# Another start address for the split left operands of a matmul chain

## The chip, the cores and the metric

The kernel runs on one core of one Trainium2 chip. The metric is the device time of one execution in microseconds. Every operand named here lies in the on-chip memory SBUF, 128 partitions wide; an address below is the byte within a partition.

## The reference

Attention between a long sequence and a short state, in both directions, followed by a two-layer network with a Mish activation. All is in float32.

```python
# x: (8, 8, 512, 64), state: (8, 8, 32, 64), w_in: (512, 2048), w_out: (2048, 512)
scores  = scale * x @ state^T;   xread = softmax(scores) @ state
scores2 = scale * state @ x^T;   sread = softmax(scores2) @ x
t   = concat([xread, sread], axis=2) -> (8 * 544, 512)
h   = t @ w_in
g   = h * tanh(log1p(exp(h)))
out = g @ w_out
```

## The kernel before, in words

A float32 product is made of three faster ones: each operand is split into a high part (a copy rounded to the type float32r) and a low part (the rest, a subtraction), and high x high, high x low and low x high are added in PSUM. The left operand is the one that is loaded into TensorE as weights (128 columns), the right one streams past it. In the trace a load is an LDWEIGHTS on the row PEld, and the streaming a MATMUL on PE.

Batch 0 is computed while the weights arrive, in an order written out as a table; batch 1 follows in a loop over eight slots of d_ff. In both, the second product (h's activation times w_out) takes 1024 columns of left operands a slot, in the tiles `gh` and `gl` of `high_g` (line 547), and streams 512 columns of w_out a matmul.

From batch 2 on the second product is done with seven products instead of eight (Winograd's form of Strassen's method). The 512 tokens of a batch are two halves p, the state rows of all batches (key "s") are one. A step is one slot j of one half: six batches of 16 steps and 8 steps of state rows, 104 in all. `combine_g` (line 662) makes the seven left operands of a step: four sums on VectorE into the tile `s`, two rounding copies on ScalarE (three blocks out of the activation tile `gu`, four out of `s`) into `gh`, and two subtractions on VectorE into `gl`. It runs one step ahead of `products` (line 684), which issues 7 x 3 matmuls of 128 x 128 weights and 256 columns, for each product on `gh`, `gh`, `gl`. The right operands are the combined parts of w_out, in the tiles `wo`, `wt23` and `wt4`. Between the steps the first product of the next batch is issued (`gemm1`: left `swh`, `swl`, right `ah`, `al`, 512 columns), and parts of the attention. The order of the steps and of what comes between them is set by lists that the program builds before it begins; on TensorE, VectorE and ScalarE instructions are issued as written.

Where the tiles lie: `gh` and `gl` have two buffers each. Since the tiles of batches 0 and 1 under the same tags are 1024 columns wide (`W`), each buffer has 4096 bytes. The two of `gh` begin at bytes 183,552 and 187,648, the two of `gl` at 191,744 and 195,840: byte 256 after a multiple of 512. So does every block of 128 columns in them. The tiles `swh` and `swl` also lie at byte 256 of 512, the right operands `wo`, `wt23`, `wt4`, `ah`, `al` and `srT` at byte 0. Batch 1 is different in one thing: its `ah` and `al` are in buffers of the tag `gu`, at byte 256.

Of the kernel before, what the change touches and what calls it, by code (L numbers as in the profile page):

```python
# [10 lines left out]
F32R = mybir.dt.float32r  # L11
# [6 lines left out]
P = 128  # L18
# [23 lines left out]
W = 1024  # L42
# [4 lines left out]
def as_f32(ap):  # L47
    return ap.bitcast(F32)
# [41 lines left out]
def state_attention_mish_kernel(ctx, tc, x_turned, x, state_wide, state, w_in, w_out, out):  # L90
# [6 lines left out]
    pool = ctx.enter_context(tc.tile_pool(name="pool", bufs=2))  # L97
# [564 lines left out]
    def combine_g(step, between=lambda: None):  # L662

        u = units.pop(step)
        key = "_".join(str(i) for i in step)
        s = pool.tile([P, 4, P], F32, tag="h", name=f"s_{key}", bufs=1)
        a21, a11, a22, a12 = (u[:, i] for i in range(4))
        dve.tensor_add(s[:, 0], a21, a22)
        dve.tensor_sub(s[:, 2], a11, a21)
        dve.tensor_sub(s[:, 1], s[:, 0], a11)  # L670
        dve.tensor_sub(s[:, 3], a12, s[:, 1])
        gh = pool.tile([P, 7, P], F32R, tag="gh", name=f"gh_{key}")
        gl = pool.tile([P, 7, P], F32R, tag="gl", name=f"gl_{key}")
        for to, of in ((slice(0, 3), u[:, 1:4]), (slice(3, 7), s)):
            act.copy(gh[:, to], of)
        between()
        for to, of in ((slice(0, 3), u[:, 1:4]), (slice(3, 7), s)):
            dve.tensor_sub(gl[:, to], of, as_f32(gh[:, to]))
        parts[step] = gh, gl
# [149 lines left out]
    for step in STEPS.split():  # L829
        what, i = re.fullmatch(r"([a-zA-Z]+)(\d*)", step).groups()  # L830
# [14 lines left out]
    key = 1  # L845
# [47 lines left out]
    for b in base:  # L893
        for j in range(4 if b == "s" else SLOTS):
            at = {2: j - LAG, "s": (-8, -5, -3, 0)[j % 4]}.get(b, min(2 * j - 8, 5))
# [25 lines left out]
    for k in range(-LAG, len(steps)):  # L921
        if k == INORDER:
            dve.on = act.on = True
        if 0 <= k < len(steps) - 1:
            combine_g(steps[k + 1], lambda: advance(k, 0))
# [3 lines left out]
        if k < 0:  # L929
            j = pending[0][1][0] // 2  # L930
            second()
            if k == -LAG:
                whole(sw_slice(2, 2, kept=kept.pop(0)))
                load_kept()
            if k == -1:
                atts[3] = attention(3)
                aTs[3] = atts[3]["aT"]
                whole(atts[3]["sc"](0))
                running.append((3, atts[3]["pieces"]()))
                xss[3] = load_x(3)  # L940
            combine_w_out(j)
            if k == -1:
                combine_g(steps[0])
            continue
        beside, loads, begun = [], [], []
        for what, b in visits.get(k, ()):
            if what[:2] == "sw":
                i = int(what[2])
# [25 lines left out]
        key, j, p = steps[k]  # L974
# [41 lines left out]
```

## Time and profile before

| what | us |
|---|---|
| median of 3 runs | 643.89 (641.83 to 643.98) |
| the profiled execution, device time | 642.11 |
| its span, first to last instruction | 640.3 |
| PE busy (matmul) | 625.7 |
| PEld busy (weight load, runs beside PE) | 539.2 |
| DVE busy (VectorE) | 492.6 |
| ACT busy (ScalarE) | 355.9 |

The durations of single matmuls in the profile overlap: a matmul's shown time includes its way through the array, and the next one starts before it has ended. The pace of a stream of matmuls is therefore read from their starts or from the length of a piece divided by its count, not from the mean time of one. All operations have line 82, that of a helper which records them; groups are told apart by their tiles. Buffer numbers are left out of the names.

### The profile page before, as it was taken

How to read it: one execution, taken by the hardware profiler on the slowest of the kernel's cores; microseconds unless marked ns; L12 is line 12 of the kernel's file. 1: busy time of each engine (PE TensorE's matmuls, PEld its weight loads, DVE VectorE, ACT ScalarE, POOL GpSimd, SP SyncE). 2: the span in 40 equal slices, each digit the busy share in tenths (PEclk: the TensorE clock that was granted, in tenths of full speed). 3: DMA queues.
4: the chain of work that ended last, by engine and by line, in shares of the span. 5: the costliest groups of instructions: out<-in, count | busy, mean ns of one | idle time of the engine just before them, and what ended most of it. 6: DMA issues, size and time to landing. Idle time of an engine off the chain costs nothing.

```text
span 640.3 us, 13377 instructions
## 1 busy us (share of the span) xinstructions
PE 625.7 (98%) x5308; PEld 539.2 (84%) x5308; DVE 492.6 (77%) x1077; ACT 355.9 (56%) x703; POOL 0.7 (0%) x6
## 2 busy tenths in 40 slices
PE   7999998999999999999999999999999999999996
PEld 5776776777778888888898888888899898899996
DVE  5989999875767676878688776878588867666685
ACT  4999773452457544654456455754465444545442
POOL 0000000000000000000000000000000000000000
PEclk9999999999999999999999999999999999999999
DMA  8977715212352243213332243224322212103100
GB/s 322 418 268 277 263 71 168 93 69 97 132 198 79 87 165 133 99 39 126 149 118 93 82 157 132 105 94 157 118 79 77 100 67 100 67 29 137 68 34 34
DMA packets 23774, 81.67 MB, mean 128 GB/s; under 512 B 4000, under 2 KB 8480, under 8 KB 18208
## 3 DMA queue, kind: packets, MB, share of 16 engines
q1 hardware_dynamic: 23424, 80.56, 34.6%
q8 instruction: 42, 0.69, 0.5%
q10 hardware_dynamic: 288, 0.26, 0.1%
q14 instruction: 20, 0.16, 0.1%
HBM read 63.50 MB, written 13.11 MB: 120 GB/s over the span
## 4 chain that ended last, share of the span: by engine, by line
PE 68%; DVE 11%; ACT 3%; issue 2%; DMA 2%; SPq 1%; DVEq 0%; ACTq 0%
PE acc L82 36%; PE ph L82 19%; PE swp L82 4%; PE ph_s L82 4%; PE acc_s L82 3%; DVE gl L82 2%; DVE s L82 2%; DVE o L82 1%; PE srp L82 1%; DVE swl L82 1%; DVE al L82 1%; ACT gh L82 1%; SPq L376 1%; PE sc L82 1%; DMA w_in<-w_in_kept 1%
## 5 line engine op out<-in xcount | busy, mean ns | idle before, releaser
L82 PE MATMUL acc<-wo,gh 128*128 128x256 f32 (+1 forms) x1024 | 230.4, 314 | 0.0
L82 PEld LDWEIGHTS acc<-wo,gh 128*128 128x128 f32 x1024 | 169.3, 190 | 28.5 <-issue 14.9
L82 PE MATMUL acc<-wo,gl 128*128 128x256 f32 (+1 forms) x512 | 158.5, 310 | 0.7 <-DVE gl L82 0.7
L82 PE MATMUL acc<-wt,gh 128*128 128x256 f32 x576 | 112.5, 283 | 0.1
L82 ACT CAST gh<-s 128x512 fp32r<-128x512 f32 x96 | 59.4, 619 | 85.3 <-DVE s L82 85.2
L82 PEld LDWEIGHTS acc<-wo,gl 128*128 128x128 f32 x512 | 97.4, 190 | 6.1 <-DVE gl L82 0.9
L82 PEld LDWEIGHTS acc<-wt,gh 128*128 128x128 f32 x576 | 89.7, 192 | 0.2 <-issue 0.2
L82 PE MATMUL acc<-wt,gl 128*128 128x256 f32 x288 | 82.9, 288 | 0.6 <-DVE gl L82 0.2
L82 PE MATMUL ph<-ah,swh 128*128 128x512 f32 (+1 forms) x260 | 80.7, 393 | 2.5 <-ACT swh L82 1.4
L82 PE MATMUL ph<-al,swh 128*128 128x512 f32 (+1 forms) x260 | 79.1, 387 | 0.0
L82 PE MATMUL ph<-ah,swl 128*128 128x512 f32 (+1 forms) x260 | 78.9, 387 | 0.0
L82 DVE TENSOR_TENSOR gl<-gu,gh 128x384 fp32r<-128x384 f32 x96 | 52.2, 544 | 34.2 <-ACT gh L82 34.2
L82 ACT CAST gh<-gu 128x384 fp32r<-128x384 f32 x96 | 49.4, 515 | 49.6 <-PE acc L82 48.0
L82 ACT ACTIVATE gu<-ph 128x256 f32<-128x256 f32 x192 | 61.0, 385 | 23.6 <-PE ph L82 23.2
L82 DVE TENSOR_TENSOR gl<-s,gh 128x512 fp32r<-128x512 f32 x96 | 66.0, 688 | 6.6 <-ACT gh L82 6.6
L82 DVE TENSOR_TENSOR swl<-swp,swh 128x512 fp32r<-128x512 f32 (+1 forms) x72 | 41.9, 623 | 22.3 <-ACT swh L82 22.2
L82 PEld LDWEIGHTS acc<-wt,gl 128*128 128x128 f32 x288 | 55.2, 192 | 3.1 <-DVE gl L82 2.5
L82 PEld LDWEIGHTS ph<-al,swh 128*128 128x128 f32 x260 | 48.4, 188 | 10.4
L82 PEld LDWEIGHTS ph<-ah,swl 128*128 128x128 f32 x260 | 48.4, 188 | 10.3
L82 PEld LDWEIGHTS ph<-ah,swh 128*128 128x128 f32 x260 | 45.1, 189 | 12.5 <-ACT swh L82 2.6
L82 ACT CAST swh<-swp 128x512 fp32r<-128x512 f32 (+1 forms) x72 | 35.3, 544 | 31.7 <-PE swp L82 31.7
L82 DVE TENSOR_TENSOR s<-gu 128x128 f32<-128x128 f32 x192 | 47.0, 286 | 5.5 <-ACT gu L82 3.3
(95 smaller groups left out, 714.3 us busy)
## 6 DMA issues: line engine op xcount, KB each, us to landing
w_in<-w_in_kept SPq DMA_DIRECT2D x24, 1024.0 KB, 5.0
wir<-in_w_in_dram SPq DMA_DIRECT2D x16, 512.0 KB, 10.3
wor<-in_w_out_dram SPq DMA_DIRECT2D x16, 512.0 KB, 9.4
x<-in_x_dram SPq DMA_DIRECT2D x8, 1024.0 KB, 4.8
out_dram<-o SPq DMA_DIRECT2D x32, 256.0 KB, 2.2
xT<-in_x_turned_dram SPq DMA_DIRECT2D x7, 1024.0 KB, 6.3
w_in_kept<-w_in SPq DMA_DIRECT2D x8, 512.0 KB, 9.8
e2T<-e2b SPq DMA_DIRECT2D x128, 32.0 KB, 1.9
```

Of the source, the lines that this page charges most:

```text
L82: made = method(*args, **kwargs)
L376: nc.sync.dma_start(e2T[s * NS:(s + 1) * NS, c].rearrange("t u g n -> t (u g n)"), turned[c * NS:(c + 1) * NS, s * 2 * P:(s + 1) * 2 * P])
```

## The change

The two tiles of `combine_g` are made 1024 columns wide, as the tiles of batches 0 and 1 are, and the 7 x 128 columns that are used begin at column 80 in `gh` and at column 48 in `gl`. With four bytes a column and buffers at byte 256 of 512, the seven blocks of `gh` then begin at byte 64 of 512 (256 + 320 = 512 + 64) and those of `gl` at byte 448 (256 + 192). No instruction is added, removed or moved on any engine or queue, and no other tile has another address.

```diff
@@ def combine_g(step, between=lambda: None):
-        gh = pool.tile([P, 7, P], F32R, tag="gh", name=f"gh_{key}")
-        gl = pool.tile([P, 7, P], F32R, tag="gl", name=f"gl_{key}")
+        gh, gl = (
+            pool.tile([P, W], F32R, tag=t, name=f"{t}_{key}")[:, at:at + 7 * P].rearrange("p (i n) -> p i n", n=P)
+            for t, at in (("gh", 80), ("gl", 48)))
```

## Rows read from the trace of the kernel before

**Rows 1.** Top of the page: span, busy us of each engine.
```profile
span 640.3 us, 13377 instructions
...
PE 625.7 (98%) x5308; PEld 539.2 (84%) x5308; DVE 492.6 (77%) x1077; ACT 355.9 (56%) x703; POOL 0.7 (0%) x6
```
**Rows 2.** Busy time by stretch: stretch, its us, engines, granted clock, DMA share, GB/s.
```profile
235.00:315.00 80.00, 79.90 (x710) 71.02 (x708) 61.00 (x149) 43.67 (x97) 0.00 (x0) 1.00 0.31 116
570.00:600.00 30.00, 30.00 (x253) 30.00 (x252) 23.52 (x61) 15.32 (x30) 0.00 (x0) 1.00 0.30 103
```
**Rows 3.** Chain that ended last, in order of time: start us, us, what.
```profile
303.56 2.75 PE ph L82 x12
306.31 5.03 PE acc L82 x42
...
602.05 7.56 PE acc L82 x63
...
615.37 18.02 PE acc_s L82 x150
```
**Rows 4.** Timeline, 226.4 to 227.4 us: start us, us, engine, line, what.
```profile
226.61 0.28 PE L82 MATMUL acc<-wt,gl 128*128 128x256 f32 x1
...
226.97 0.28 PE L82 MATMUL acc<-wo,gl 128*128 128x256 f32 x1
226.97 0.31 PEld L82 LDWEIGHTS acc<-wo,gh 128*128 128x128 f32 x2
```
**Rows 5.** Timeline of PE in batch 1, 512 columns a matmul.
```profile
104.23 0.39 PE L82 MATMUL acc<-wo,gl 128*128 128x512 f32 x1
...
104.91 0.39 PE L82 MATMUL acc<-wo,gl 128*128 128x512 f32 x1
```
**Rows 6.** Groups from 225.9 to 228 us: count, busy us, mean ns, idle before.
```profile
L82 PEld LDWEIGHTS acc<-wo,gh 128*128 128x128 f32 x6 | 0.9, 192 | 0.0
...
L82 PE MATMUL acc<-wt,gh 128*128 128x256 f32 x6 | 1.2, 283 | 0.0
```
**Rows 7.** Timeline of PE, first and ninth matmul of a stretch behind a wait.
```profile
221.12 0.40 PE L82 MATMUL acc<-wt,gh 128*128 128x256 f32 x2
...
222.07 0.28 PE L82 MATMUL acc<-wo,gl 128*128 128x256 f32 x1
```
**Rows 8.** Groups of that stretch, 221.1 to 222.1 us.
```profile
L82 PE MATMUL acc<-wo,gh 128*128 128x256 f32 x4 | 0.8, 281 | 0.0
...
L82 PEld LDWEIGHTS acc<-wo,gh 128*128 128x128 f32 x5 | 0.8, 189 | 0.0
```
**Rows 9.** Groups from 225.64 to 225.7 us, batch 3's first product and what follows.
```profile
L82 PE MATMUL ph<-ah,swl 128*128 128x512 f32 x1 | 0.4, 389 | 0.0
L82 PE MATMUL acc<-wo,gh 128*128 128x256 f32 x1 | 0.3, 277 | 0.0
```
**Rows 10.** Tiles gh and gl: ns min/median/max; below, who waited (us, times).
```profile
L82 PE MATMUL acc<-wt,gh x576: 277/283/356, 183.8 to 609.2; 128*128 128x256 f32 x192
L82 ACT CAST gh<-s x96: 613/620/625, 170.5 to 605.0; 128x512 fp32r<-128x512 f32 x96
L82 DVE TENSOR_TENSOR gl<-gu,gh x96: 495/551/559, 170.6 to 605.1; 128x384 fp32r<-128x384 f32 x96
L82 DVE TENSOR_TENSOR gl<-s,gh x96: 677/691/694, 171.2 to 605.6; 128x512 fp32r<-128x512 f32 x96
...
  PEld acc L82: 3.4, 11
```
**Rows 11.** Timeline of PE, eight transposes of 128 columns.
```profile
519.52 1.04 PE L82 MATMUL srTp<-ident,srds 128*128 128x128 f32 x8
```
**Rows 12.** Groups from 222.6 to 224.1 us, the beginning of batch 3's first product.
```profile
L82 PE MATMUL ph<-ah,swh 128*128 128x512 f32 x2 | 0.6, 396 | 0.0
```
**Rows 13.** The page's groups: VectorE's sums ahead of gh and gl.
```profile
L82 DVE TENSOR_TENSOR s<-gu 128x128 f32<-128x128 f32 x192 | 47.0, 286 | 5.5 <-ACT gu L82 3.3
```
**Rows 14.** Groups from 98 to 140 us, batch 1's first product.
```profile
L82 PE MATMUL ph<-ah,swh 128*128 128x512 f32 x16 | 4.9, 389 | 0.0
```

## The prediction, made before the changed kernel ran

> **What bounds the kernel now.** I read the page's totals first, then the busy time by stretch, the chain of waits, the timeline of TensorE, and last the view of the tiles gh and gl. The totals [rows 1] show PE busy for 98% of 640.3 us, DVE for 77%, ACT for 56%. An average says little, so the stretches [rows 2]: from 235 to 315 us PE is busy 79.90 of 80 us and DVE 61.00, and from 570 to 600 us PE all of it, with a granted clock of 1.00 in both, the upper of its two levels (2.4 GHz). In batches 2 to 7 and in the state rows, PE is the only engine without air. The chain of waits agrees [rows 3]: from 303.56 us it runs on PE alone, in pieces of the first and of the second product, and its last piece of matmuls is 150 of the second product in 18.02 us. So the time of this part is a count of matmuls times their pace.
>
> **The pace.** 150 matmuls in 18.02 us are 120.1 ns each; 42 in 5.03 us are 119.8, and 63 in 7.56 us 120.0 [rows 3]. In the timeline the first matmul on gl comes every 0.36 us, three matmuls [rows 4]. A 512-column matmul of batch 1 with the same left tiles comes every 0.68/3 = 227 ns [rows 5]. The difference, 107 ns, is what 256 columns cost; 120 - 107 = 13 ns per matmul are something else. Every one of these matmuls is paired with a weight load of 128 columns that runs under the matmul before it: in [rows 4] a load starts with the matmul ahead of it, and it shows 192 ns where the pace is 120 [rows 6].
> [...]
>
> That the 13 ns are not fixed is shown by the matmuls that are not in the steady run. From 221.12 us, just behind a wait, eight matmuls go from 221.12 to 222.07 us, 119 ns each in the view's hundredths [rows 7], and in that stretch the loads show 189 ns and the matmuls 281 [rows 8], against 192 and 283 in the steady stretch [rows 6]. The first 256-column matmul behind a 512-column one shows 277 ns [rows 9]. The shortest on these tiles is 277, the median 283 [rows 10]. Of a matmul's shown time a constant part is its way through the array: 283 goes with a pace of 120, and 389 with 227, so 163 and 162 ns. By that, 277 is a pace of 114, and 281 one of 118. Same shapes, same addresses: what differs is how the load's and the matmul's reads fall against each other. That is what makes a change of address worth a forecast at all.
>
> **The change, part by part.** It adds no instruction, removes none, and moves none: each engine's order is the same. Tiles gh and gl of batch 2 on become 1024 wide and use columns 80 to 975 and 48 to 943. Their slots were already 4096 bytes, because batches 0 and 1 put 1024 columns there, so no other tile shifts. The left operand of 104 steps x 21 = 2184 matmuls (six batches of 16 steps and 8 steps of state rows; seven products of three matmuls a step) starts at byte 64 or 448 of a 512-byte row of addresses where it started at 256. The right operands stay at 0.
> - Writes of gh by ACT and of gl by DVE: same shape, other start. The rows of gh<-s, gl<-gu and gl<-s range from 613 to 625, 495 to 559 and 677 to 694 ns [rows 10]. I take zero. Bounds: their spread, at most 64 ns on a DVE op. It is hidden by PE: DVE has 24% of air from 235 to 315 us [rows 2]; were that gone, a step's 0.06 us would be 104 x 0.06 = 6 us. I put nothing of this in the sum.
> - The weight loads and the matmuls under them: the whole effect. No row has a 128-column load of these products from byte 64 or 448, so I bound it. Best row: 277 ns, 6 ns below the median. 2184 x 6 = 13.1 us less. Lower still is the row of the eight transposes (srTp): 1.04 us less the 0.163 of the way through the array, by eight, is 110 ns each, with a load of 128 columns each [rows 11]; they are transposes of 128 columns, so this is the far end: 2184 x 10 = 21.8 us. Worst row: the first two 512-column matmuls of a first product, on ah and swh, have a mean of 396 where the settled one has 389 [rows 9, 12], 7 ns more: 2184 x 7 = 15.3 us more.
> - Value taken: 4 ns less, halfway between the drifting stretch (2 ns less) and the first matmul behind a long one (6 ns less), since both are the same instruction as the one in question, and neither is nearer. 2184 x 4 = 8.7 us. About 1 in 20 of these matmuls stands behind a wait and would not gain; that is 0.4 us, left within the range.
> - How much arrives at the end: all of it, as long as PE stays the bound. One step is 21 x 120 = 2.52 us of PE; DVE's part of it is four sums of 0.286 [rows 13] and the two subtractions of 0.551 and 0.691 [rows 10], 2.39 us. With 116 ns PE needs 2.44, still above DVE in a run of steps without a first product between. At 114 ns it is 2.39, and DVE would be late next, at the gl that opens a product; the present waits there are 3.4 us in 11 times [rows 10]. In batches 2 to 7 the first product gives DVE room between (2.75 us before two steps, [rows 3]), so I take no loss at 4 ns. What lies behind the last matmul (633.4 to 640.3 us) stays.
>
> Sum: the profiled execution took 642.11 us (span 640.3). 642.11 - 8.7 = 633.4. The median of the three runs shown, 643.89, is 1.8 above it, so 635.2: **635 us**.
>
> **The rivals.**
> *Same.* The start address does not matter, and the pace has 120 for a reason that lies elsewhere. For it: batch 1 takes its right operands (ah, al) from slots at byte 256 where the other batches take them from byte 0, with the left ones at 256 in both; the 16 matmuls of its first product in the row show 389 ns [rows 14], and the settled row of batch 3's shows 389 too [rows 9]. That is a move of 256 bytes between the two reads that did nothing. If the pattern repeats in 64 bytes, 64, 256 and 448 are one place. Against it: 277, 281 and 283 for one kind of instruction [rows 8 to 10] say the reads do get into each other's way. Result 643.9, give or take the 2 us of the runs.
> The Trainium skill (TensorE: Matmul & The Clock Gate, "Step-by-step: what each phase is for") says that PE has two independent read ports and that loading the next weights takes no read bandwidth from the running matmul. By that rule this change does nothing and this rival holds; the trace speaks against it so far as loads and matmuls lengthen together [rows 6, 8].
> *Slower.* The two reads meet more often than now. Place: the load of the next gh or gl under a running matmul. Price: the matmul takes the 7 ns more that rows of the first product show [rows 12], 2184 x 7 = 15 us, 659 us. It decides when the new start makes the moving read wait for one more of these steps per load; half of it, 3 ns, gives 650. For it: 396 occurs with the same kind of operands, and a high part and a low part now have different starts, so the run of loads has three distances and no longer one. Against it: these 396 stand only until the stream has settled, and 256-column matmuls settle below.
> *Faster, by more.* The meeting goes away wholly: 114 ns or less. 2184 x 6 gives 630.8, with the transposes' 110 it would be 622 less what DVE then holds up, some 626.
>
> **How the numbers follow.** About 0.5% (3.2 us) is what a measurement of this kernel can tell from no change. Gain of 3.2 to 11 us (2 to 5 ns): 0.36. Gain over 11 us: 0.16. Same: 0.32. Slower by over 3.2 us: 0.16. So faster 0.52, same 0.32, slower 0.16. The likeliest is faster, its own range 628 to 640. The range 628 to 646 leaves out the gains over 16 us (0.06) and the losses over 2 us above the median (0.14 at most).
>
> **What would show it.** Right: the 150 matmuls at the end in 17.4 us instead of 18.02, a median of 279 for the matmuls on gh and gl, loads of 188 instead of 192 ns, first-product rows unchanged at 389 to 396, and waits of PE for gl of no more than 5 us. Same would show 18.02 and 283 again. Slower would show 286 or more. It would be wrong in its reason, though right in its number, if the pace stayed at 120 and waits went instead, or if ACT's and DVE's rows for gh and gl changed by more than their spread.

## The result, and the profile after

| | us |
|---|---|
| the kernel before, median of 4 runs | 643.50 (641.83 to 643.98) |
| the changed kernel, median of 4 runs | 636.61 (635.38 to 637.03) |
| ratio, with its 95% interval | 0.9894 (0.9871 to 0.9918) |
| profiled execution of the changed kernel | 637.03, span 635.2 |

The change takes 6.9 us off. The top of the page, span and busy us of each engine:

```profile
span 635.2 us, 13377 instructions
...
PE 617.3 (97%) x5308; PEld 529.2 (83%) x5308; DVE 492.5 (78%) x1077; ACT 356.0 (56%) x703; POOL 0.7 (0%) x6
```

Against [rows 1], matmuls are 8.4 us less busy and weight loads 10.0 us; VectorE and ScalarE have the work they had. Then the view of the tiles gh and gl (ns min/median/max; the last two lines are who waited for them, us and times):

```profile
L82 PEld LDWEIGHTS acc<-wt,gh x576: 186/188/191, 185.2 to 604.6; 128*128 128x128 f32 x192
L82 PE MATMUL acc<-wt,gh x576: 276/276/358, 185.3 to 604.7; 128*128 128x256 f32 x192
L82 ACT CAST gh<-s x96: 612/620/624, 172.0 to 600.8; 128x512 fp32r<-128x512 f32 x96
L82 DVE TENSOR_TENSOR gl<-gu,gh x96: 494/550/560, 172.1 to 600.9; 128x384 fp32r<-128x384 f32 x96
L82 DVE TENSOR_TENSOR gl<-s,gh x96: 677/691/694, 172.6 to 601.4; 128x512 fp32r<-128x512 f32 x96
...
  PEld acc L82: 7.4, 19
...
  PE acc L82: 3.7, 14
```

The median matmul was 283 ns and the shortest 277 [rows 10]; now the shortest, 276, is the median. The loads went from 192 ns [rows 6] to 188. ScalarE's and VectorE's rows for the same tiles have not moved. What grew is the wait for gl: the weight loads wait 7.4 us in 19 times, where it was 3.4 in 11 [rows 10], and the matmuls themselves 3.7 us in 14 times, where it was 0.9 in 2.

The chain that ended last, pieces of it (start us, us, what):

```profile
304.05 2.75 PE ph L82 x12
306.80 4.78 PE acc L82 x42
...
597.96 7.16 PE acc L82 x63
...
610.87 7.06 PE acc_s L82 x62
...
618.54 0.63 ACT gh_s L82
...
619.19 0.70 DVE gl_s L82
...
619.91 0.71 DVE s_s L82 x3
...
620.65 0.30 DVE s_s L82
...
620.97 0.63 ACT gh_s L82
```

42 matmuls take 4.78 us, 113.8 ns each, where they took 5.03 [rows 3]; 63 take 7.16, 113.7 each. The 12 matmuls of a first product take 2.75 us as before. But the chain no longer runs to its end on PE. From 618 us it goes round a loop: copy on ScalarE (0.63), subtraction on VectorE (0.70), the next step's sums (0.71 + 0.30), the next copy. From one copy's start to the next are 620.97 - 618.54 = 2.43 us a step; 21 matmuls at 114 ns take 2.39. This loop costs little: in the state rows the loads wait for gl once, 0.3 us.

How the 6.9 us come about can be worked out from the starts of the single matmuls in the two traces. From the start of a matmul on gh or gl to the next start on PE, where no wait lies between (under 160 ns), the mean fell from 119.7 ns (2095 of them) to 114.3 (2082): 5.4 ns, times 2090 is 11.3 us. The gaps over 160 ns hold, beyond 115 ns each, 11.5 us in the trace before and 16.2 us after: 4.7 us are given back. 11.3 - 4.7 = 6.6; from the first matmul of batch 2's second product to the start of the last matmul the trace after is 6.65 us shorter (451.80 to 445.15).

Where it is given back shows when both traces are cut at the halves of the batches, 168 of these matmuls each, for which the pace alone would give 0.9 us. The first halves of batches 3 to 6, in which VectorE is busy for 80 to 81%, got only 0.1 us shorter each; there the loads' wait for gl grew from 0.2 us (once) to 1.0 us (three times) in each. The second halves of batches 2 to 6 got 0.6 to 0.7 us shorter. The two halves of batch 7, in which VectorE is busy for 70 and 73% and no load waits for gl, got 1.0 and 1.1 us shorter. Who waited for gl in the first half of batch 3, before (261.81 to 295.77 us) and after (262.37 to 296.23 us; us in total, times, longest):

```profile
PEld acc L82 <- DVE gl L82: 0.2, 1, 0.2
...
PEld acc L82 <- DVE gl L82: 1.0, 3, 0.4
```

The span fell by 5.1 us only, since the profiled execution reached batch 2 later by 1.5 us. That lies ahead of everything that the change touches; from 80 to 155 us the granted clock was 0.98 in this execution, where it was 1.00 in the one before. That stretch before and after, and a later one after (columns as in [rows 2]):

```profile
80.00:155.00 75.00, 72.33 (x579) 55.78 (x578) 64.52 (x117) 37.75 (x75) 0.00 (x0) 1.00 0.28 94
...
80.00:155.00 75.00, 72.31 (x572) 55.73 (x571) 62.91 (x116) 37.34 (x74) 0.00 (x0) 0.98 0.28 92
...
235.00:315.00 80.00, 79.36 (x713) 70.01 (x712) 62.21 (x154) 43.75 (x98) 0.00 (x0) 1.00 0.33 122
```

### The profile page after: what moved, and what is told of

Same layout as the page of the kernel before. It is cut to its first block, busy times and chain, and to the rows that moved or that the text cites. A ratio compares the mean times of both kernels' runs of the same rounds, so it can differ in the third digit from the quotient of the medians.

```text
span 635.2 us, 13377 instructions
## 1 busy us (share of the span) xinstructions
PE 617.3 (97%) x5308; PEld 529.2 (83%) x5308; DVE 492.5 (78%) x1077; ACT 356.0 (56%) x703; POOL 0.7 (0%) x6
## 4 chain that ended last, share of the span: by engine, by line
PE 52%; DVE 20%; ACT 7%; issue 4%; DMA 2%; SPq 1%; DVEq 0%; ACTq 0%
PE acc L82 26%; PE ph L82 14%; DVE gl L82 4%; DVE s L82 4%; PE swp L82 4%; PE ph_s L82 4%; DVE swl L82 3%; DVE o L82 3%; ACT gh L82 2%; PE acc_s L82 2%; ACT scs L82 2%; ACT L82 1%; PE srp L82 1%; DVE al L82 1%; SPq L376 1%
## 5 line engine op out<-in xcount | busy, mean ns | idle before, releaser
L82 PE MATMUL acc<-wo,gh 128*128 128x256 f32 (+1 forms) x1024 | 226.3, 310 | 0.0
L82 PEld LDWEIGHTS acc<-wo,gh 128*128 128x128 f32 x1024 | 166.7, 188 | 28.6 <-issue 15.1
L82 PE MATMUL acc<-wt,gh 128*128 128x256 f32 x576 | 109.0, 278 | 0.1
L82 PEld LDWEIGHTS acc<-wt,gh 128*128 128x128 f32 x576 | 87.2, 188 | 0.3 <-issue 0.3
L82 PE MATMUL acc<-wt,gl 128*128 128x256 f32 x288 | 81.2, 282 | 1.9 <-DVE gl L82 1.9
```

Source lines behind the costliest of these rows:

```text
L82: made = method(*args, **kwargs)
```

## The experiments

Two questions were open: which of the two starts does it, and where the other five microseconds went. "Pace" below is the mean from one matmul on gh or gl to the next, waits left out, as above.

### Which start does it

**High parts alone.**

```diff
-            for t, at in (("gh", 80), ("gl", 48)))
+            for t, at in (("gh", 80), ("gl", 0)))
```

> Only the high parts move (to byte 64 of 512), the low parts stay at byte 256. Theory A, each load by itself: a matmul is held up by the load that runs under it, by where that load's bytes begin. Then the matmuls with a gh load under them (two of three) run at 113 to 114 ns and those with a gl load at 120: per product of three 347, loads of gh near 188 ns and of gl near 192, and about two thirds of the change's gain (4 to 5 us less than before). Theory B, the pair: the gain comes from high and low parts having different starts, so that one load's start differs from the one before. Then the pace is that of the whole change, 340 per three. Theory C, only one of the two moves does something: all of the gain or none of it here, and the reverse with the low parts alone.

**Low parts alone.**

```diff
-            for t, at in (("gh", 80), ("gl", 48)))
+            for t, at in (("gh", 0), ("gl", 48)))
```

> Only the low parts move (to byte 448 of 512), the high parts stay at byte 256. Theory A: one of three matmuls runs at 113 to 114 ns, two at 120: 354 per three, and 2 to 3 us less than before. Theory B: 340 per three, as with the whole change. Theory C: all or nothing, the reverse of the run with the high parts alone.

**Both at byte 64.**

```diff
-            for t, at in (("gh", 80), ("gl", 48)))
+            for t, at in (("gh", 80), ("gl", 80)))
```

> High and low parts both at byte 64 of 512. Theory A (each load by itself): if byte 448 is no special place, the same pace as the change, 113 to 114 ns; the profile's medians of the matmuls on gh and gl are both 276. Theory B (the difference between high and low is what helps): 120 ns and 283 again, as before, since the two have the same start, as they had before.

One run each, beside a run of the kernel before of 643.35 us: 639.29, 639.12 and 638.09 us. From the tile views of the three, in this order, matmuls on the high and on the low parts with the right operand in wt. Single times this close cannot be ranked; the reading rests on the traces:

```profile
L82 PE MATMUL acc<-wt,gh x576: 277/281/353, 183.2 to 606.7; 128*128 128x256 f32 x192
L82 PE MATMUL acc<-wt,gl x288: 279/281/388, 183.5 to 606.8; 128*128 128x256 f32 x144
```
```profile
L82 PE MATMUL acc<-wt,gh x576: 276/282/356, 183.8 to 606.7; 128*128 128x256 f32 x192
L82 PE MATMUL acc<-wt,gl x288: 276/278/389, 184.0 to 606.8; 128*128 128x256 f32 x144
```
```profile
L82 PE MATMUL acc<-wt,gh x576: 276/281/355, 183.2 to 605.6; 128*128 128x256 f32 x192
L82 PE MATMUL acc<-wt,gl x288: 276/281/388, 183.4 to 605.7; 128*128 128x256 f32 x144
```

The paces are 118.0, 117.8 and 117.1 ns, of 119.7 before and 114.3 with the whole change. None of the theories holds as it was put. Theory A wanted two kinds of matmul in the first run, 114 and 120; all three of a product are near 118 (118.0, 118.4 and 117.6 by the load underneath). In the second run the one that is fast, at 115, is the matmul on gl, under which the next gh is loaded from byte 256; the one with the load from 448 under it has 119.6. So a load's start shows in later matmuls too, or the load that counts is not only the one that starts with the matmul: a load shows 188 to 192 ns, longer than the 114 to 120 from one matmul to the next. Theory B wanted 120 with both at 64, and it is 117; theory C wanted all or nothing. What the three show together: either move alone is worth about 2 ns; of the pairs tried so far the last 3 came only with both moved, to different starts.

**A start for every step.** (`done_steps` is a list that is empty at first.)

```diff
-            for t, at in (("gh", 80), ("gl", 48)))
+            for t, at in (("gh", 16 * (len(done_steps) % 8)), ("gl", 16 * (len(done_steps) % 8))))
+        done_steps.append(step)
```

> Every step takes another start, high and low parts alike: 256, 320, 384, 448, 0, 64, 128, 192 of 512, 13 steps each. Theory A says that the pace of a step depends on its start: steps at 256 show 120 ns, steps at 64 and 448 show 113 to 114, and the six other places tell how wide the bad place is. If the start does not matter by itself (theory B), all steps show 120. In all it should lie between the kernel before and the change: 637 to 643 us.

641.87 us. The state rows' steps follow each other without a first product between for the first six, with starts 256, 320, 384, 448, 0 and 64. From the timeline of PE, the first matmul of each step (start us, us, what):

```profile
615.09 0.40 PE L82 MATMUL acc_s<-wo,gh_s 128*128 128x256 f32 x2
...
617.61 0.39 PE L82 MATMUL acc_s<-wo,gh_s 128*128 128x256 f32 x2
...
620.00 0.40 PE L82 MATMUL acc_s<-wo,gh_s 128*128 128x256 f32 x2
...
622.48 0.40 PE L82 MATMUL acc_s<-wo,gh_s 128*128 128x256 f32 x2
...
624.96 0.40 PE L82 MATMUL acc_s<-wo,gh_s 128*128 128x256 f32 x2
...
627.48 0.40 PE L82 MATMUL acc_s<-wo,gh_s 128*128 128x256 f32 x2
...
629.88 0.40 PE L82 MATMUL acc_s<-wo,gh_s 128*128 128x256 f32 x2
```

The differences, by 21 matmuls:

| start, byte of 512 | 256 | 320 | 384 | 448 | 0 | 64 |
|---|---|---|---|---|---|---|
| us for the step | 2.52 | 2.39 | 2.48 | 2.48 | 2.52 | 2.40 |
| ns a matmul | 120 | 114 | 118 | 118 | 120 | 114 |

In this table 0 and 256, and 64 and 320, which are 256 bytes apart, agree. Over all 104 steps the matmuls that have the load of a high part under them, with no change of start between, say the same of all four such pairs, within about 1 ns: 119.5 and 119.5 ns at 0 and 256, 116.7 and 116.1 at 64 and 320, 118.9 and 119.9 at 128 and 384, 118.0 and 117.4 at 192 and 448. The start matters by itself (theory A), and the old place is the worst of the eight or next to it; but 448, which theory A had expected at 113 to 114, shows 118. Steps finer than 64 bytes were not tried. At 64 and 320 the stream has two settled paces, 113 to 114 and 117 to 118, and goes from one to the other; hence 114 in the single step above and 117 in the run with both at 64.

**Another pair, and the pair exchanged.** Two tests of what is left, that the pattern has a period of 256 bytes and that the pair helps by being apart.

```diff
-            for t, at in (("gh", 80), ("gl", 48)))
+            for t, at in (("gh", 80), ("gl", 112)))
```

> High parts at byte 64 as in the change, low parts at 192 instead of 448. The run with a start for every step showed the same pace at starts that are 256 bytes apart (120 at 0 and 256, 117 at 64 and 320, 117 at 192 and 448). If the pattern repeats every 256 bytes, 64 with 192 is the same as 64 with 448: a median of 276 and a pace of 113 to 115, and the change's time. If it repeats in 512 only, the pace is another, between 115 and 120.

```diff
-            for t, at in (("gh", 80), ("gl", 48)))
+            for t, at in (("gh", 48), ("gl", 80)))
```

> The change with the two starts exchanged: high parts at byte 448, low parts at 64. If what helps is that high and low parts lie half of 256 bytes apart (64 and 192 of 256), the order is all the same: a median of 276 and a pace of 113 to 115. If the direction counts (the load of high parts behind that of low ones), the pace lies between 115 and 118.

635.70 us (before: 641.95) and 634.95 us (before: 642.42); paces 114.2 and 114.7. The tile views of the two:

```profile
L82 PE MATMUL acc<-wt,gh x576: 276/276/356, 184.2 to 603.4; 128*128 128x256 f32 x192
```
```profile
L82 PE MATMUL acc<-wt,gh x576: 276/276/353, 183.1 to 602.7; 128*128 128x256 f32 x192
```

Low parts at 192 do what they do at 448, and with 64 and 448 which of the two sorts has which start makes a difference of 0.4 ns. Both expectations, of the period and of the pair, hold. Pairs that are apart by something other than 128 of 256 bytes (except 64, in the two runs with one move) were not tried.

### Where the other five microseconds went

**Lighter sums, with and without the change.** The four sums of a step are replaced by two that are twice as wide. These two kernels compute something else than the reference; they serve only to take work off VectorE.

```diff
-        dve.tensor_add(s[:, 0], a21, a22)
-        dve.tensor_sub(s[:, 2], a11, a21)
-        dve.tensor_sub(s[:, 1], s[:, 0], a11)
-        dve.tensor_sub(s[:, 3], a12, s[:, 1])
+        dve.tensor_add(s[:, :2], u[:, :2], u[:, 2:])
+        dve.tensor_sub(s[:, 2:], u[:, :2], u[:, 2:])
```

> The change, with the four sums of a step (128 columns each) replaced by two of 256 columns: another computation, VectorE has some 0.3 us less per step (two of 416 ns for four of 286). The theory that the matmuls' faster pace is partly given back to VectorE: 2183 matmuls at 114.3 instead of 119.7 ns are 11.8 us, of which 6.9 arrive; with VectorE lighter 3 us or more of the missing 5 should come too: 634 us or less, and the waits of weight loads for gl fall from 7.4 us to under 4. The rival, that the missing microseconds are lost elsewhere (the first two batches, transfers): no further gain, 636 to 637.

> The same replacement of the sums in the kernel before (starts at byte 256). There TensorE is the bound in batches 2 to 7 with waits for gl of 3.4 us in all, so lighter sums alone should give 0 to 2 us: 641 to 643.5 us, pace 120 as before. If this gains as much as in the change (3 us or more), VectorE was a bound of its own before, and the two effects only add.

With the change 628.82 us (627.70 to 630.48), ratio to before 0.9799 (0.9761 to 0.9837); without it 637.42 (637.16 to 638.03), ratio 0.9927 (0.9899 to 0.9954), both against 641.95. Between the two lie 8.6 us, where the change alone is worth 6.9. In the traces the difference from batch 2's second product to the start of the last matmul is 447.80 - 437.65 = 10.15 us, where it was 6.65 with the sums as they were and the pace gives 11.6 (5.5 ns, 2106 times). The wait for gl and one piece of the chain, without the change:

```profile
  PEld acc L82: 0.7, 2
...
304.26 5.03 PE acc L82 x42
```

and with it:

```profile
  PEld acc L82: 0.9, 2
...
302.40 4.78 PE acc L82 x42
```

The pace is not touched by the sums (119.8 and 114.3), and the waits for gl are nearly gone in both. So most of the missing microseconds are VectorE's: with its work lighter by 0.3 us a step, 3.5 us more of the pace arrive in the traces, and 1.7 us more by the medians. What holds back the rest was not traced. The expectation for the change held (634 or less, waits under 4 us), though 4.5 of the microseconds come with lighter sums alone. The expectation for the kernel before was wrong: 4.5 us is more than 0 to 2, and VectorE had been a second bound there already.

**Sums one step ahead.** A cure that computes the reference: each step's sums, moved into a function `sums`, are issued a step earlier into the other half of the tile, while VectorE waits for ScalarE's copy. The place where they are issued (the rest of the edit is left out here):

```diff
         for to, of in ((slice(0, 3), u[:, 1:4]), (slice(3, 7), s)):
             act.copy(gh[:, to], of)
+        if following in units:
+            sums(following)
         between()
```

> The change, and each step's four sums are issued one step earlier on VectorE, into the other half of a two-part tile, in the time in which VectorE waits for ScalarE's copy of the same step; the computation is the reference's. If what is given back is the chain sums, copy of gh, subtraction to gl, next sums (2.43 us per step against 2.39 of matmuls), the state rows' steps lose their waits and the whole gains 2 to 4 us over the change: 632.5 to 634.5. If VectorE's sheer amount of work in batches 3 to 6 is the limit, the gain is only at the state rows: 1 to 2 us.

634.66 us (633.09 to 634.70), ratio to before 0.9876 (0.9847 to 0.9905). That is 2 us less than the change by the medians and 1 us by the ratios, and the intervals overlap: no clear gain, and just above the 632.5 to 634.5 expected. The chain shows that the loop at the end is cut:

```profile
608.91 19.20 PE acc_s L82 x168
```

All 168 matmuls of the state rows at 114.3 ns, without a wait. In batches 3 to 7 each half is shorter by 0 to 0.6 us, but batch 2's first half took 43.01 us for 41.95, perhaps since VectorE combines the last pieces of w_out there; that was not traced. The next run leaves most of batch 2 out (its edit is against the run just shown):

```diff
-            combine_g(steps[k + 1], lambda: advance(k, 0), steps[k + 2] if k + 2 < len(steps) else None)
+            combine_g(steps[k + 1], lambda: advance(k, 0), steps[k + 2] if base[3] - 2 <= k < len(steps) - 2 else None)
```

> As the run with the sums one step ahead, but only from the end of batch 2 on: in batch 2 the earlier sums cost 1 us (its first half took 43.01 instead of 41.95 us), since VectorE combines the last pieces of w_out there. So 1 us less than that run: 633 to 634 us, and the state rows' 168 matmuls in 19.2 us again.

635.65 us (633.56 to 635.95), ratio 0.9888 (0.9873 to 0.9902): not the 633 to 634 expected. Batch 2's loss is gone in the trace (42.17), and the first half of batch 3 is 0.8 us longer instead. Sums earlier settle the state rows' loop, worth 0.3 us; in the batches VectorE's amount of work stays what it was, and the loads still wait 6.5 and 6.9 us for gl, of 7.4 in the change.

### The same for the first product

```diff
+        pad(16)
+        hi = part("swh")
+        pad(32)
+        lo = part("swl")
```

These are the main lines of the edit. Here `pad` leaves that many columns of four bytes free ahead of the next tiles, once.

> The change, and the left operands of the first product too: the tiles swh begin at byte 64 of 256, swl at 192 (they began at 0 of 256), from batch 1 on, by unused columns between the tiles. If the bad start costs 512-column matmuls what it costs 256-column ones, the first product's matmuls fall from 227 to 236 ns to some 220, 672 of them: 4 to 6 us of TensorE's time, of which half may arrive: 633 to 635 us. If the load, which covers only half of a 512-column matmul, does not hold it up, there is no change: 636 to 637 us.

638.73 us (638.08 to 639.42), ratio 0.9943 (0.9928 to 0.9959): 2 us slower than the change by the medians, 3 by the ratios. Neither branch of the expectation had this. In the chain the 12 matmuls of a first product, 2.75 us after the change, are now

```profile
252.50 2.79 PE ph L82 x12
```

and from matmul to matmul the mean of its 667 went from 228.7 to 232.7 ns. The pair of places that is good under 256 columns is worse under 512 than the old one. The second product also got slower, 114.9 instead of 114.3; why was not tested.

> The change with the sums ahead from the end of batch 2 on, and with swh and swl at bytes 64 and 192 of 256. If both parts do what is hoped for, their gains add, and VectorE's waits limit the sum: 630 to 632.5 us. If the first product's start does nothing, 633 to 634 us, as with the sums alone.

This is the sums ahead from batch 2's end on and the first product's new starts in one kernel: 636.82 us (635.52 to 638.26), ratio 0.9910 (0.9895 to 0.9924). That is above both expectations; the first product's matmuls take 232.7 ns here too. No version that computes the reference was clearly faster than the change.

## Why the prediction was right, and which of its terms were off

It said 635 us, faster, by a faster pace of the matmuls on gh and gl at the same number of instructions; measured are 636.61. The mechanism that it named, the pace by the address, is what the runs show. That the total came so close is partly luck, since two terms were off in opposite directions.

- *What bounds.* Half right. "PE is the only engine without air" was read from a busy row of 79.90 of 80 us [rows 2]. A matmul's shown time goes on for some 163 ns after the next one could start, so waits shorter than that leave no hole in the row; a matmul behind a wait shows as a longer one (the maximum of 356 in [rows 10]). With lighter sums the kernel before gains 4.5 us: VectorE was a bound beside PE already.
- *The pace.* Right in kind: the 13 ns over what 256 columns cost were not fixed, and a change of address alone takes 5.4 of them away. Its reason, that the load's and the matmul's reads meet, is not shown by any run. That the drifting stretch and the first matmul behind a long one [rows 7 to 9] were the same effect is borne out as far as the numbers go: 277 was the shortest before, 276 is the median after, and 281, the drifting stretch, is the median of the high parts in the runs with these alone, and with both sorts, at byte 64.
- *Value taken: 4 ns less.* Mis-sized: 5.4 ns. The nearer row was the 277 ns of [rows 9], not the middle between it and the stretch.
- *How much arrives: all of it.* Mis-sized the other way. At 114 ns the prediction itself had VectorE late next, but it took no loss, since in batches 2 to 7 "the first product gives DVE room between". In the first halves of batches 3 to 6 that was not enough: they gained 0.1 us each of 0.9. Among its signs were waits for gl of no more than 5 us; the weight loads wait 7.4 us (the matmuls themselves 3.7), and by the starts 4.7 us were given back. Of the step-by-step sum the time of a step's parts (2.39 us) was right, but its loop, copy to subtraction to sums to copy, takes 2.43. The two errors, 3 us more and 5 us less, cancel in part: 8.7 us were forecast and 6.9 came.
- *Writes of gh and gl at nothing.* Right: their rows agree within 1 ns in the median.
- *What would show it.* The loads at 188 ns and the first product unchanged were found; the median is 276 for 279. The piece of 150 matmuls in 17.4 us does not stand in the chain, whose end is now VectorE's and ScalarE's loop, but the matmuls themselves did what was forecast: from the first to the 150th start of the state rows' matmuls are 17.34 us after and 17.89 before, one wait of 0.3 us included. They are not the last ones, as the prediction has it: before, the chain left PE at 633.4 us, and 18 more matmuls ran until 635.5 us beside the output's sums.
- *The rival that nothing changes* rested on batch 1, whose right operands lie 256 bytes off with no other pace [rows 14]. The observation was right, and a variant of its second reading (a pattern that repeats in 64 bytes) came true for the left operands: the pattern repeats, but in 256 bytes. If that holds for the right operands too (no run moved them by less), a move of 256 could show nothing. It is no evidence about a move of 64. The rule of the Trainium skill behind that rival (TensorE: Matmul & The Clock Gate, "Step-by-step: what each phase is for"), two independent read ports and no read bandwidth taken from the running matmul, does not carry over to the time of these streams: with the columns, the order and the counts the same, the start of the loaded operand moves the pace between 113 and 120 ns. Whether the load takes something from the running matmul or is itself slower from some starts, the runs do not tell.
- *The slower rival* did not come about here, but a start that slows a stream exists: the new starts of the first product cost 4 ns more a matmul. That this is more meetings of the two reads is not shown.

What the mechanism is inside the engine stays open. The runs show that the starts of the loaded operands matter, in steps of 64 bytes with a period of 256, and that the same start can have two settled paces; they do not show whether the start counts by itself or by its distance from that of the right operand, which stayed at byte 0 of 512 for the second product in every run.

## What to carry to other kernels

Where a matmul stream is bound by its own pace and a weight load runs under every matmul, look at the pace against the cost of its columns; if it is some nanoseconds more, try other start addresses within 256 bytes for the loaded operands. One kernel with a start for every step gives a map of single starts; pairs of starts have to be tried by themselves. The good place has to be looked for anew at each shape: the one found here for 256 columns was worse at 512. Then ask what the faster stream will meet: here 4.7 of 11.3 us were given back, most of it to an engine that showed 76% busy. Do not take a full PE row for proof that nothing else waits.

## What the runs showed that was not expected

- The pace depends on the start of the loaded operand with a period of 256 bytes: 120 ns at 0 and 256, 113 to 114 or 117 to 118 at 64 and 320, 118 to 120 at 128 and 384, 117 to 118 at 192 and 448.
- Two kinds of load with different starts (64 with 192, and 64 with 448 either way round) run at 114 to 115 ns; no run with a single start for both held that.
- A pair of starts that is good for 256 columns (64 with 192 of 256) makes 512-column matmuls slower, 232.7 instead of 228.7 ns.
- The faster pace is given back mainly in four halves of batches, where the wait for gl grew from 0.2 to 1.0 us each, and not in the loop on which the chain ends.
